# First loads of an attention and soft-MoE kernel split over two kinds of DMA queue, with products of zeros in TensorE's waits

## The chip, the cores and the metric

The kernel runs on one core of a Trainium2 chip. The metric is the device time of one execution in microseconds (us). Five runs of the kernel before gave a median of 154.34 us (153.34 to 154.71).

## The reference, cut to what matters

There are two stages. The first is attention over 4 batches of 8 heads, 768 tokens and 64 channels; each head is causal ("retrieval") or keeps only the first 4 tokens and a window of 64:

```python
scores = scale * np.matmul(q, k.transpose(0, 1, 3, 2))
mask = np.where(retr[0, :, 0, 0, None, None], full_mask, stream_mask)
scores = np.where(mask[None, :, :, :], scores, -1000000000.0)
a = softmax(scores)                      # over the last axis
attn_out = np.matmul(a, v)
```

The second takes the 3072 tokens x 512 channels that come out as `x` and runs a soft mixture of 8 experts with 4 slots each:

```python
logits = x @ phi                                        # 512 x 32
slot_input = softmax(logits, axis=0).T @ x              # 32 slots
slot_out[e] = np.maximum(slot_input[e] @ w1[e], 0.0) @ w2[e]   # 512 x 1024 x 512
out = softmax(logits, axis=1) @ slot_out
```

All inputs are float32 in HBM: q, k and v are 6.3 MB each, w1 and w2 16.8 MB each; the output is 6.3 MB.

## The kernel before, in words

**Attention.** The work goes by pairs of heads, n = 0 to 15 (four pairs a batch). A pair's q, k and v come as tiles of 96 partitions x 2 heads x 512 values: partition p holds tokens 8p to 8p+7. TensorE transposes them (`transpose`, line 73: 16 small products into one PSUM tile), an engine copies them out (`evac`, line 82), and v is turned back into token blocks (`v_blocks`). Within a pair the causal blocks are split into six groups (line 23). For each group g the loop issues the scores (`qk`, line 106: TensorE, then the exponential on ScalarE), and between them a list written out by hand (lines 413 to 474): masks on VectorE, the products with v (`pvmm`), the transposes of the next pair, and once per pair the division by the row sums (`norm`). The order on each engine is the order in which the program issues; nothing is moved by a scheduler. Group 0 of a pair needs only the token blocks 0 to 2 of q and 0 and 1 of k. Partitions 0 to 47 of a raw tile hold the blocks 0 to 2, partitions 48 to 95 the blocks 3 to 5.

**Loads.** From pair 1 on, loads are issued by GpSimd (`load`, line 65), whose DMAs can turn float32 into bfloat16 on the way (the queue that the profile calls software_dynamic, here SWDGE). They go three pairs ahead, into three buffers for each of q, k and v; one load must wait until the transposes of the pair that used its buffer are done. Between them GpSimd issues the sixteen weight loads of 2 MB each (`w_load`, line 271), about three for four pairs, and the six that are left at pair 13. At most eight of GpSimd's DMAs are outstanding: the ninth waits for the first. All of this is one queue.

**Pair 0** is different: `load_first` (line 55) has SyncE and ScalarE issue its loads (queues called hardware_dynamic, here HWDGE). [...]q, k and v land as float32 in memory that later holds the weights w2[7] and w2[6], and `cast` (line 363) turns them into bfloat16 on VectorE and ScalarE (lines 372 to 375 and 390). The flags `is_retrieval` come by ScalarE's queue (`ri`, line 327). While the data is on its way TensorE runs 20 products of a tile of zeros (`warm`, line 59), and 3 more after the first transposes; they write a scratch tile in PSUM that nobody reads. VectorE meanwhile computes what the masks of all heads are made from; `head_mask(h)` then makes head h's mask, for heads 0 and 1 in group 0, for the others at places listed in `MASK_AT`.

**The end.** After pair 15 the last token logits, `exp_tokens` and `slots_in` (lines 484 to 507) give the slots' inputs `siT`. `layer1` (512 x 1024 for each expert) and `layer2` follow on TensorE (lines 510 to 566), then the output: 24 products with `slot_out` (line 585), scaled on ScalarE and VectorE and written to HBM by SyncE (line 591) in nine DMAs.

Of the kernel before, what the change touches and what calls it, by code (L numbers as in the profile page):

```python
# [10 lines left out]
F32 = mybir.dt.float32  # L11
BF16 = mybir.dt.bfloat16
# [7 lines left out]
P = 128  # L20
# [9 lines left out]
MCOL = [0, None, 256]  # L30
NG = len(GROUPS)

MASK_AT = {(0, 1): 2, (0, 2): 3, (0, 3): 4, (0, 4): 5, (1, 1): 6, (1, 2): 7}


class Attn:
# [16 lines left out]
        self.xb, self.xT, self.expB, self.elg, self.lg = {}, {}, {}, {}, {}  # L53

    def load_first(self, w, eng, stage):
        self.rawt[w, 0] = self.raw.tile([P, 2, 512], BF16, tag=w + "r", name=w + "r")
        eng.dma_start(stage, self.src[w][0, 0:2].rearrange("h (p s) d -> p h (s d)", s=8))

    def warm(self, count):

        t = self.trp.tile([P, 256], F32, tag="tr", name="warm")
        for _ in range(count):
            self.nc.tensor.matmul(t, self.zeros[:, :P], self.zeros, start=True, stop=True)

    def load(self, n, which="qkv"):
        b, h = n // 4, 2 * (n % 4)
# [15 lines left out]
    def evac(self, n, w):  # L82
        tp = self.tp.pop((w, n))
        pool = self.vTp if w == "v" else self.qkT
        dst = pool.tile([P, 768], BF16, tag=w + "T", name=w + "T")
        o = dst.rearrange("c (j s p) -> c j s p", j=6, s=8)
        i = tp.rearrange("c (s j p) -> c j s p", j=6, s=8)
        if n == 0 and w == "q":
            self.nc.scalar.copy(o, i)
        else:  # L90
            self.nc.vector.tensor_copy(o, i)  # L91
        self.T[w, n] = dst

    def v_blocks(self, n):
# [149 lines left out]
def kernel(  # L244
# [24 lines left out]
    w2s = [singles.tile([P, 8, DM], BF16, name=f"w2_{e}") for e in range(NE)]  # L269
# [27 lines left out]
    with ExitStack() as actx:  # L297
        asing = actx.enter_context(tc.tile_pool(name="asing", bufs=1))
# [5 lines left out]
        ri = asing.tile([P, 2 * H], I32, name="ri")  # L304
# [16 lines left out]
        stage = [stage[:96, 1024 * i:1024 * (i + 1)].rearrange("p (h c) -> p h c", h=2) for i in range(2)]  # L321
        stage.append(w2s[NE - 2].rearrange("p a b -> p (a b)").bitcast(F32)[:96, :1024].rearrange(
            "p (h c) -> p h c", h=2))
# [7 lines left out]
        at.zeros = at.ptp.tile([P, 2, 512], BF16, tag="pT", name="zeros").rearrange("p a c -> p (a c)")[:, :256]  # L331
        nc.vector.memset(at.zeros, 0.0)
# [30 lines left out]
        def cast(w, i, part, eng):  # L363
            o, x = at.rawt[w, 0][:96, :, part], stage[i][:, :, part]
            if eng is nc.scalar:
                eng.copy(o, x)
            else:
                eng.tensor_copy(o, x)  # L368

        lo, hi = slice(0, 256), slice(256, 512)  # L370
# [13 lines left out]
        def head_mask(h):  # L384
            for c0, c1, r in ((0, 256, r0), (256, 640, r1)):
                nc.vector.tensor_scalar(msk[:, h, c0:c1], level[:, c0:c1], r[:, h:h + 1], 2.0,
                                        op0=ALU.add, op1=ALU.is_ge)

        at.evac(0, "k")
        cast("v", 2, slice(0, 512), nc.vector)  # L390
        wi = 0
        for n in range(NP):
            if n + 3 < NP:
# [14 lines left out]
            for g in range(NG):  # L408
                at.qk(n, g)
                last = n == NP - 1  # L410

                b, bt = (n - 4) // 4, (n - 4) % 4 if n >= 4 else 0
                if g == 0:
                    if n == 0:
                        at.transpose(0, "v")
                        head_mask(0)
                        at.evac(0, "v")
                        head_mask(1)

                        nc.vector.tensor_scalar(fb0, r0, 1.0, 30000.0, op0=ALU.subtract, op1=ALU.mult)  # L420
                        nc.vector.tensor_scalar(fb1, r1, 1.0, 30000.0, op0=ALU.subtract, op1=ALU.mult)
                    else:
                        at.pvmm(n - 1, 4)
                        at.v_blocks(n)
                        at.evac_blocks(n)
                    at.mask(n, 0)
                elif g == 1:
                    if n:
                        at.pvmm(n - 1, 5)
                    else:  # L430
                        at.v_blocks(n)
                        at.evac_blocks(n)
# [7 lines left out]
                elif g == 2:  # L440
                    if not last:
                        at.transpose(n + 1, "q")
                    at.pvmm(n, 0)
                    at.mask(n, 1)
                    if not last:
                        at.evac(n + 1, "q")
                elif g == 3:
                    if not last:
                        at.transpose(n + 1, "k")
                    at.pvmm(n, 1)  # L450
                    at.mask(n, 2)
                    if not last:
                        at.evac(n + 1, "k")
# [32 lines left out]
        at.x_transpose(n, range(3))  # L486
        at.evac_x(n, range(3))
        at.pvmm(n, NG - 1)
        at.norm(n, 1)
# [7 lines left out]
        at.token_logits(b, 1, range(3), (at.scp, "sc"))  # L497
        at.exp_tokens(b, 0, range(1))
        at.x_transpose(n, range(3, 6))
        at.evac_x(n, range(3, 6))  # L500
        at.slots_in(sip, b, range(3))
# [1 line left out]
        at.exp_tokens(b, 1, range(1))  # L503
        for c in range(2):
            at.exp_tokens(b, c, range(1, 4))
        at.slots_in(sip, b, range(3, 6))
        nc.vector.tensor_copy(siT, sip)
        hs, hT = {}, {}

        def layer1(e4, c):  # L510
# [59 lines left out]
    with tc.tile_pool(name="osb", bufs=8) as osb, \  # L570
         tc.tile_pool(name="ops", bufs=6, space=PSUM) as ops:
        for b in range(B):
# [4 lines left out]
            r = 0  # L577
# [50 lines left out]
```

The softmax here doesn't subtract the row's maximum and nothing guards it: scores larger than these inputs give would overflow.

## Time and profile before

| what | value |
|---|---|
| median of five runs | 154.34 us (153.34 to 154.71) |
| the profiled execution's own time | 154.49 us |
| its span, first to last instruction | 152.8 us |
| outside the span | 1.7 us |
| TensorE busy | 129.5 us (85%) |
| VectorE busy | 116.3 us (76%) |
| ScalarE busy | 112.5 us (74%) |
| first scores of pair 0 | at 9.37 us |
| slots' inputs `siT` ready for layer 1 | at 120.2 us |
| read from HBM | 52.5 MB |

The page gives busy time for each engine, the span in 40 slices with a digit for the busy tenths (`PEclk` is the TensorE clock that was granted, in tenths of full speed, `DMA` the busy share of the 16 DMA engines, `GB/s` what they wrote), DMA queues, the chain of work that ended last, and groups of instructions. A float32 that is turned into bfloat16 on the way counts with the bytes that are written, so 200 GB/s of such loads are 400 GB/s of reading.

### The profile page before, as it was taken

To read this page: it belongs to the slowest core of one execution; us is meant where nothing else is said; L and a number is where in the kernel's file an instruction comes from. 1 tells how busy PE (TensorE), PEld (TensorE's weight loads), DVE (VectorE), ACT (ScalarE), POOL (GpSimd) and SP (SyncE) were. 2 spreads that over 40 slices of the span, in tenths; PEclk is the share of its full clock that TensorE was granted. 3 is DMA by queue.
4 is the path that set the end of the run, shared out by engine and by line. 5 is a ranking of instruction groups with operands and counts; after the bars stand their busy time and mean duration, and the time that the engine had idled before them with its cause. 6 is when DMAs were issued, how large, how long until landed. Compare 5 with 4: busy or idle time off the path is not lost.

```text
span 152.8 us, 5568 instructions
## 1 busy us (share of the span) xinstructions
PE 129.5 (85%) x2398; PEld 86.7 (57%) x2398; DVE 116.3 (76%) x284; ACT 112.5 (74%) x176; POOL 40.5 (26%) x75
## 2 busy tenths in 40 slices
PE   7789989999799999999999999999977799399000
PEld 5546656667576675767667577766646348244000
DVE  6279799899988899898899989989976143189400
ACT  3146889999899899899989899989984262169200
POOL 7543563514336132433523335400000000000000
PEclk9999999999999999999999999999999699969975
DMA  4999999999999999999999999999999998149995
GB/s 118 226 209 208 228 191 229 198 227 193 214 222 195 227 195 228 195 215 220 198 224 200 221 194 214 225 212 217 219 212 214 214 214 172 36 173 405 412 418 240
DMA packets 14423, 33.51 MB, mean 219 GB/s; under 512 B 1856, under 2 KB 10496, under 8 KB 12480
## 3 DMA queue, kind: packets, MB, share of 16 engines
q0 software_dynamic: 11808, 25.63, 88.2%
q1 hardware_dynamic: 2240, 7.14, 12.8%
q10 hardware_dynamic: 352, 0.40, 1.0%
q8 instruction: 18, 0.29, 0.7%
q14 instruction: 5, 0.04, 0.1%
HBM read 52.50 MB, written 6.29 MB: 385 GB/s over the span
## 4 chain that ended last, share of the span: by engine, by line
DMA 53%; DVE 16%; PE 16%; issue 5%; POOL 2%; DVEq 0%; ACT 0%; ACTq 0%; POOLq 0%
DMA w<-in_moe_w_dram 33%; DMA kr<-in_k_dram 9%; DMA qr<-in_q_dram 7%; DMA ri<-in_is_retrieval_dram 4%; PE pv L149 4%; PE sc L114 4%; DVE ot L590 4%; DVE xb L162 3%; PE tpv L78 2%; DVE pT L136 2%; PE op L585 2%; DVE pT L133 2%; DVE vb L103 1%; POOL w L279 1%; DVE xT L176 1%
## 5 line engine op out<-in xcount | busy, mean ns | idle before, releaser
L123 ACT ACTIVATE pT<-sc,fb 128x512 bf16<-128x512 f32 (+1 forms) x96 | 52.6, 620 | 4.3 <-PE sc L114 2.9
L119 ACT ACTIVATE pT<-sc 128x1024 bf16<-128x1024 f32 (+1 forms) x48 | 44.8, 952 | 5.6 <-PE sc L114 4.9
L149 PE MATMUL pv<-vb,pT 128*128 128x65 bf16 x672 | 37.3, 196 | 3.9 <-DVE pT L133 2.3
L114 PE MATMUL sc<-qT,kT 64*128 64x256 bf16 (+3 forms) x320 | 36.0, 288 | 0.2 <-DVE kT L91 0.2
L149 PEld LDWEIGHTS <-pT 128*128 128x128 bf16 x672 | 26.6, 98 | 15.2 <-issue 6.3
L136 DVE TENSOR_TENSOR pT<-pT,msk 128x1024 bf16<-128x1024 bf16 (+1 forms) x32 | 19.7, 616 | 0.0
L162 DVE TENSOR_TENSOR xb<-pv,rs 128x384 bf16<-128x384 f32 x32 | 17.9, 558 | 1.1
L69 POOL DMA_DIRECT2D qr<-in_q_dram x15 | 9.7, 650 | 32.5 <-PE tpq L78 30.0
L114 PEld LDWEIGHTS <-kT 64*128 64x128 bf16 x320 | 10.4, 94 | 8.0 <-issue 1.5
L176 DVE COPY xT<-tpx 128x768 bf16<-128x768 bf16 (+1 forms) x17 | 9.1, 534 | 4.4 <-PE tpx L170 4.3
L69 POOL DMA_DIRECT2D vr<-in_v_dram x15 | 9.4, 630 | 10.7 <-PE tpv L78 10.7
L69 POOL DMA_DIRECT2D kr<-in_k_dram x15 | 9.5, 636 | 7.8 <-PE tpk L78 7.5
L133 DVE TENSOR_TENSOR pT<-pT,msk 128x1024 bf16<-128x1024 bf16 x16 | 10.9, 681 | 0.0
L78 PE MATMUL tpq<-ident,qr 96*64 96x96 bf16 x256 | 9.2, 218 | 1.0 <-DVE qr L368 1.0
L170 PE MATMUL tpx<-ident,xb 128*128 128x128 bf16 x96 | 8.2, 220 | 1.9 <-DVE xb L162 1.1
L91 DVE COPY vT<-tpv 128x768 bf16<-128x768 bf16 x16 | 8.8, 547 | 1.3 <-PE tpv L78 1.3
L78 PEld LDWEIGHTS <-qr 96*64 96x64 bf16 x256 | 6.9, 116 | 4.0 <-issue 2.5
L590 DVE TENSOR_SCALAR ot<-op,rrow 128x512 f32<-128x512 f32 (+1 forms) x13 | 8.6, 723 | 0.7 <-PE op L585 0.5
L78 PE MATMUL tpk<-ident,kr 96*64 96x96 bf16 x256 | 9.1, 218 | 0.0
L78 PE MATMUL tpv<-ident,vr 96*64 96x96 bf16 x256 | 9.1, 217 | 0.0
L103 DVE COPY vb<-tpb 128x768 bf16<-128x768 bf16 x16 | 8.9, 557 | 0.2 <-PE tpb L97 0.2
L78 PEld LDWEIGHTS <-vr 96*64 96x64 bf16 x256 | 6.9, 116 | 3.8 <-issue 3.4
(88 smaller groups left out, 158.0 us busy)
## 6 DMA issues: line engine op xcount, KB each, us to landing
w<-in_moe_w_dram POOLq DMA_DIRECT2D x15, 1024.0 KB, 14.7
out_dram<-ot SPq DMA_DIRECT2D x7, 768.0 KB, 6.3
qr<-in_q_dram POOLq DMA_DIRECT2D x15, 192.0 KB, 10.5
kr<-in_k_dram POOLq DMA_DIRECT2D x15, 192.0 KB, 9.8
vr<-in_v_dram POOLq DMA_DIRECT2D x15, 192.0 KB, 9.3
w<-in_moe_w_dram POOLq DMA_DIRECT2D x2, 512.0 KB, 33.9
out_dram<-ot SPq DMA_DIRECT2D x1, 512.0 KB, 2.7
w<-in_k_dram ACTq DMA_DIRECT2D x1, 384.0 KB, 5.7
```

The source lines that it names most:

```text
L69: self.nc.gpsimd.dma_start(t[:96], self.src[w][b, h:h + 2].rearrange("h (p s) d -> p h (s d)", s=8))
L78: self.nc.tensor.transpose(tp[64 * i:64 * (i + 1), s * 96:(s + 1) * 96], src[:96, i, s * 64:(s + 1) * 64], self.ident[:96, :96])
L103: self.nc.vector.tensor_copy(self.vbufs[n % 2][:, :, :, :64], tp.rearrange("p (j h d) -> p h j d", j=6, h=2))
L114: nc.tensor.matmul(sc[:, hh, c:c + ni * P], kT[po:po + 64, j * P:(j + 1) * P], qT[po:po + 64, i0 * P:(i0 + ni) * P], start=True, stop=True)
L119: nc.scalar.activation(pT[:, :, :L], sc[:, :, :L], ACT.Exp, scale=self.scale)
L123: nc.scalar.activation(pT[:, hh, :L], sc[:, hh, :L], ACT.Exp, scale=self.scale, bias=fb[:, h + hh:h + hh + 1])
L133: nc.vector.tensor_mul(v, v, m)
L136: nc.vector.tensor_mul(pT[:, :, :L], pT[:, :, :L], self.msk[:, h:h + 2, c:c + L])
L149: self.nc.tensor.matmul(self.pv[n, lo][:, hh, i % 3, :], pT[:, hh, o:o + P], vb[:, hh, j, :65], start=first, stop=True, skip_group_check=True)
L162: nc.vector.tensor_mul(xo, pv[:, :, :, :64], rs.to_broadcast([P, 2, 3, 64]))
L176: self.nc.vector.tensor_copy(self.xT[n // 4][:, n % 4, c], self.tp.pop(("x", n))[:, c])
L590: nc.vector.tensor_scalar_mul(ot[:, i, c0:c0 + cl], op[:, :cl], rr)
```

## The change

- `load_first` is called for q and k only. It loads partitions 0 to 47 (token blocks 0 to 2) of q by SyncE and of k by ScalarE, as float32 into staging memory, and partitions 48 to 95 by GpSimd, which casts on the way. These two GpSimd DMAs stand ahead of everything on its queue but the two iotas; the building of `ident` (a memset and a select) comes after them.
- v of pair 0 is loaded by GpSimd with `load`, ahead of pair 1. Its staging memory and its cast are gone, and so is the cast of the second half of q and k. `ri` moves from ScalarE's queue to SyncE's, behind q.
- The transposes of q and k of pair 0 come in two halves of 48 partitions (`transpose_first`, `evac_first`): the first halves before the loop, with 4 products of zeros after them instead of 3; the second halves in group 0, after the first scores, with 2 products of zeros after them. v's transposes move from group 0 to group 1 and its token blocks from group 1 to group 2; 2 more products of zeros stand in group 1. The masks of heads 2 to 7 move by one group.
- Before the loop VectorE's copy of kT no longer stands behind the instructions that read the flags.
- Products of zeros write a PSUM tile of their own (`waste`), so that they no longer wait for a copy.
- At the end the scores of the last batch's tokens with the first three of the four channel blocks of the first half move up ahead of the transposes of pair 15, and 10 products of zeros are spread over the waits up to layer 1.

```diff
-MASK_AT = {(0, 1): 2, (0, 2): 3, (0, 3): 4, (0, 4): 5, (1, 1): 6, (1, 2): 7}
+MASK_AT = {(0, 2): 2, (0, 3): 3, (0, 4): 4, (1, 1): 5, (1, 2): 6, (1, 3): 7}
...
+        t = self.raw.tile([P, 2, 512], BF16, tag=w + "r", name=w + "r")
+        src = self.src[w][0, 0:2].rearrange("h (p s) d -> p h (s d)", s=8)
+        eng.dma_start(stage, src[:48])
+        self.nc.gpsimd.dma_start(t[:48], src[48:96])
+        self.rawt[w, 0] = t
+
+    def transpose_first(self, w, late):
+        src, p0, n = self.rawt[w, 0], 0 if late else 64, 48
+        tp = self.trp.tile([P, 8 * n], BF16, tag="tr", name="tp" + w)
+        for s in range(8):
+            for i in range(2):
+                self.nc.tensor.transpose(tp[64 * i:64 * (i + 1), s * n:(s + 1) * n],
+                                         src[p0:p0 + n, i, s * 64:(s + 1) * 64],
+                                         self.ident[p0:p0 + n, p0:p0 + n])
+        self.tp[w, 0] = tp
...
-        at.load_first("q", nc.sync, stage[0])
-        at.load_first("k", nc.scalar, stage[1])
-        at.load_first("v", nc.sync, stage[2])
-        nc.scalar.dma_start(ri, bass.AP(tensor=ir32, offset=0, ap=[[0, P], [1, 2 * H]]))
         nc.gpsimd.iota(ki, pattern=[[0, 1]], base=0, channel_multiplier=1)
...
+        at.load_first("q", nc.sync, stage[0])
+        at.load_first("k", nc.scalar, stage[1])
+        nc.sync.dma_start(ri, bass.AP(tensor=ir32, offset=0, ap=[[0, P], [1, 2 * H]]))
...
+        at.load(0, "v")
         at.load(1)
         at.load(2)
...
-        cast("q", 0, lo, nc.vector)
-        cast("q", 0, hi, nc.vector)
-        cast("k", 1, lo, nc.scalar)
-        cast("k", 1, hi, nc.vector)
-        at.transpose(0, "q")
-        at.transpose(0, "k")
-        at.warm(3)
-        at.evac(0, "q")
+        nc.vector.tensor_copy(at.rawt["q", 0][64:112], stage[0])
+        nc.scalar.copy(at.rawt["k", 0][64:112], stage[1])
+        for w in "qk":
+            at.transpose_first(w, False)
+        at.warm(4)
+        at.evac_first("q", False, nc.scalar.copy)
+        at.evac_first("k", False, nc.vector.tensor_copy)
...
-        at.evac(0, "k")
-        cast("v", 2, slice(0, 512), nc.vector)
...
                     if n == 0:
-                        at.transpose(0, "v")
+                        for w in "qk":
+                            at.transpose_first(w, True)
+                            at.evac_first(w, True, nc.vector.tensor_copy)
+                        at.warm(2)
                         head_mask(0)
-                        at.evac(0, "v")
                         head_mask(1)
...
-        at.token_logits(b, 0)
+        at.token_logits(b, 0, range(3))
         at.token_logits(b, 1, range(3), (at.scp, "sc"))
+        at.x_transpose(n, range(3))
+        at.evac_x(n, range(3))
+        at.pvmm(n, NG - 1)
+        at.norm(n, 1)
+        at.waste = at.pvp.tile([P, 256], F32, tag="pv0", name="waste")
+        at.warm(2)
+        at.token_logits(b, 0, range(3, 4))
         at.exp_tokens(b, 0, range(1))
+        at.warm(4)
```

More of the change, by code (lines that the diff above doesn't have):

```diff
@@ L55, in load_first, with evac_first, warm @@
     def load_first(self, w, eng, stage):
[L56 to L61, printed above, removed]
+        t = self.raw.tile([P, 2, 512], BF16, tag=w + "r", name=w + "r")
[12 more added lines that the diff above has]
+        self.tp[w, 0] = tp
+    def evac_first(self, w, late, eng):
+        tp = self.tp.pop((w, 0))
+        if not late:
+            self.T[w, 0] = self.qkT.tile([P, 768], BF16, tag=w + "T", name=w + "T")
+        dst = self.T[w, 0][:, 384:] if late else self.T[w, 0][:, :384]
+        eng(dst.rearrange("c (j s p) -> c j s p", j=3, s=8), tp.rearrange("c (s j p) -> c j s p", j=3, s=8))
+    def warm(self, count, cols=256):
         for _ in range(count):
-            self.nc.tensor.matmul(t, self.zeros[:, :P], self.zeros, start=True, stop=True)
+            self.nc.tensor.matmul(self.waste[:, :cols], self.zeros[:, :P], self.zeros[:, :cols],
+                                  start=True, stop=True)
     def load(self, n, which="qkv"):
@@ L87, in evac @@
         i = tp.rearrange("c (s j p) -> c j s p", j=6, s=8)
[L88 to L91, printed above, removed]
+        self.nc.vector.tensor_copy(o, i)
         self.T[w, n] = dst
@@ L320 @@
         stage = w2s[NE - 1].rearrange("p a b -> p (a b)").bitcast(F32)
-        stage = [stage[:96, 1024 * i:1024 * (i + 1)].rearrange("p (h c) -> p h c", h=2) for i in range(2)]
-        stage.append(w2s[NE - 2].rearrange("p a b -> p (a b)").bitcast(F32)[:96, :1024].rearrange(
-            "p (h c) -> p h c", h=2))
-        at.load_first("q", nc.sync, stage[0])
-        at.load_first("k", nc.scalar, stage[1])
-        at.load_first("v", nc.sync, stage[2])
-        nc.scalar.dma_start(ri, bass.AP(tensor=ir32, offset=0, ap=[[0, P], [1, 2 * H]]))
+        stage = [stage[64:112, 1024 * i:1024 * (i + 1)].rearrange("p (h c) -> p h c", h=2) for i in range(2)]
         nc.gpsimd.iota(ki, pattern=[[0, 1]], base=0, channel_multiplier=1)
@@ L330 @@
         nc.gpsimd.iota(qi, pattern=[[128, 2], [1, 8], [8, 16]], base=0, channel_multiplier=0)
-        at.zeros = at.ptp.tile([P, 2, 512], BF16, tag="pT", name="zeros").rearrange("p a c -> p (a c)")[:, :256]
+        at.load_first("q", nc.sync, stage[0])
+        at.load_first("k", nc.scalar, stage[1])
+        nc.sync.dma_start(ri, bass.AP(tensor=ir32, offset=0, ap=[[0, P], [1, 2 * H]]))
+        at.zeros = asing.tile([P, 256], BF16, name="zeros")
+        at.waste = at.pvp.tile([P, 256], F32, tag="pv1", name="waste")
         nc.vector.memset(at.zeros, 0.0)
@@ L361 @@
         nc.vector.tensor_single_scalar(sink, kk, float(n_sink), op=ALU.is_lt)
[L363 to L370, printed above, removed]
-        cast("q", 0, lo, nc.vector)
-        cast("q", 0, hi, nc.vector)
-        cast("k", 1, lo, nc.scalar)
-        cast("k", 1, hi, nc.vector)
-        at.transpose(0, "q")
-        at.transpose(0, "k")
-        at.warm(3)
-        at.evac(0, "q")
+        nc.vector.tensor_copy(at.rawt["q", 0][64:112], stage[0])
[5 more added lines that the diff above has]
+        at.evac_first("k", False, nc.vector.tensor_copy)
         nc.vector.tensor_single_scalar(rne, ri.rearrange("p (h c) -> p h c", c=2), 0.0, op=ALU.not_equal)
@@ L430 @@
                     else:
-                        at.v_blocks(n)
-                        at.evac_blocks(n)
+                        at.transpose(0, "v")
+                        at.evac(0, "v")
+                        at.warm(2)
                     if bt == 1:
@@ L440 @@
                 elif g == 2:
+                    if n == 0:
+                        at.v_blocks(n)
+                        at.evac_blocks(n)
                     if not last:
@@ L485 @@
         at.pvmm(n, NG - 2)
[L486 to L489, printed above, removed]
         sip = at.scp.tile([P, 4, ES], F32, tag="sc", name="sip")
@@ L495 @@
                              skip_group_check=True)
-        at.token_logits(b, 0)
+        at.token_logits(b, 0, range(3))
         at.token_logits(b, 1, range(3), (at.scp, "sc"))
+        at.x_transpose(n, range(3))
[3 more added lines that the diff above has]
+        at.waste = at.pvp.tile([P, 256], F32, tag="pv0", name="waste")
+        at.warm(2)
+        at.token_logits(b, 0, range(3, 4))
         at.exp_tokens(b, 0, range(1))
+        at.warm(4)
         at.x_transpose(n, range(3, 6))
@@ L505 @@
             at.exp_tokens(b, c, range(1, 4))
+        at.warm(2)
         at.slots_in(sip, b, range(3, 6))
         nc.vector.tensor_copy(siT, sip)
+        at.warm(2)
         hs, hT = {}, {}
```

## The prediction, made before the changed kernel had run

> **What bounds the kernel now.** I read the page's slices first. TensorE, VectorE and ScalarE have idle tenths everywhere; the DMA row has none from the second slice to the 33rd.
>
> ```profile
> PEclk9999999999999999999999999999999699969975
> DMA  4999999999999999999999999999999998149995
> ...
> q0 software_dynamic: 11808, 25.63, 88.2%
> ```
>
> Then the chain that ended last, in order of time, and the waits of TensorE near the end:
>
> ```profile
> 97.90 34.68 DMA w<-in_moe_w_dram
> 132.58 0.04 issue
> 132.62 0.32 PE sp L545 x4
> ```
>
> ```profile
> PE sp L545 <- DMA w<-in_moe_w_dram: 2.1, 1, 2.1
> ```
>
> GpSimd issues its last weight load at 97.90 us; it lands 34.68 us later, at 132.58, because everything queued before it has to pass. TensorE is through with all that it has at 130.5 and waits 2.1 us for it. Nothing that follows can start earlier: last products, `slot_out`, output, 20.2 us to the end at 152.8. So the time is: the moment at which the input stream has passed, plus 20.2, plus 1.7 outside the span (154.49 in all; the median of the runs is 0.15 less). The inputs are the same bytes before and after. An edit counts only if it moves the end of that stream, or the 20.2 behind it. Attention is covered by 2.1 us of waiting; it gains nothing by being earlier.
>
> The stream is therefore looked at where it isn't full: its start. The DMA queues up to 6.6 us:
>
> ```profile
> q1 hardware_dynamic: 374, 0.73, 45.8%
> q10 hardware_dynamic: 298, 0.40, 21.9%
> ...
> qr<-in_q_dram POOLq DMA_DIRECT2D x2, 192.0 KB, 7.6
> ```
>
> and the first issues and products, from the timeline:
>
> ```profile
> 0.81 0.38 SPq L57 DMA_DIRECT2D w<-in_q_dram  x1
> ...
> 1.12 4.45 PE L63 MATMUL warm<-zeros 128*128 128x256 bf16 x20 [1.12 <-DVE zeros L332]
> ...
> 1.84 0.81 POOL L69 DMA_DIRECT2D qr<-in_q_dram  x1
> ...
> 6.62 0.87 PE L78 MATMUL tpq<-ident,qr 96*64 96x96 bf16 x16 [1.04 <-DVE qr L368]
> ...
> 9.37 0.61 PE L114 MATMUL sc<-qT,kT 64*128 64x256 bf16 x4 [0.20 <-DVE kT L91]
> ...
> 19.83 0.53 PE L78 MATMUL tpq<-ident,qr 96*64 96x96 bf16 x16
> ```
>
> There is no row for q0, GpSimd's queue: in 6.6 us it moved nothing, though its first DMA was issued at 1.84. All of the first 1.13 MB is HWDGE, and it is slow: the windows show 356 GB/s from 3 to 4 us, but 272, 230 and 173 in the next three.
>
> **The change, part by part.**
>
> *The stream.* Before: the first q0 load (192 KB, issued 1.84) lands 7.0 us after its issue, at 8.9. At the 187 to 210 GB/s of the windows from 7 to 10 us it takes 0.95 us, and a landing shows about 0.9 us after the last packet; so q0 starts at about 7.0 on an average engine, as HWDGE's 1.16 MB end. After: HWDGE has only 0.40 MB. By the windows that amount is through at 3.7 us (16 + 152 KB to 3.0, then 356 GB/s). The 0.77 MB moved to q0 write 384 KB, at 200 GB/s 1.9 us. If q0 starts when HWDGE is done, the place reached at 7.0 before is reached at 3.7 + 1.9 = 5.6 to 5.8: a gain of 1.2 us.
>
> Two things can spoil it. One is GpSimd's issuing. Iotas end at 1.37; two loads at 0.81 and 0.64 end at 2.85; `ident` (memset and select, 1.33 to 1.89 before) 0.56; v is issued at 3.4. If a load's packets come 1.0 us after its 0.64 of issuing, v's come at 5.05, while the two half loads (0.95 together) are through at 4.75: a gap of 0.3, and with 2 us from issue to packets 0.7. I take 0.3. The other is when q0 can start at all. The Trainium skill (DMA: Bandwidth & Descriptors, Latency and other measured facts) gives a first byte of about 1 us for SWDGE; the row says 4.8 us or more (issue 1.84, nothing by 6.6). By the rule q0 is ready at about 2.4 to 3.2, so the gain is whole; by the row, taken as a latency, q0 starts at 1.4 + 4.8 = 6.2, the DMA engines stand idle from 3.7 to 6.2, and the place is reached at 8.1 to 8.3: a loss of 1.2. I take the rule's side, since the trace has a reason for the late start: q0 appears just as v's last HWDGE packets leave, and the DMA share dips only to 0.81 between. A start hidden behind a full queue looks like this; a latency that ends just there would be chance. But one trace can't exclude it.
>
> So the stream: -1.2 + 0.3 = -0.9 us, between -1.2 and +1.3.
>
> *Behind the stream.* TensorE will reach its wait some 2 us earlier than before (below) and the last weights come only 0.9 earlier, so it stands idle longer and in two pieces. Before, the clock fell to 0.52 only in the window from 133 to 134, after the last 12 of the L545 products. After, I expect those to run at half clock. The price from the same kernel: 16 products of L516 take 1.90 us at clock 0.50 and 1.05 at full; so `slot_out`, which starts 0.34 after the first product, starts 0.3 later. From -0.1 (the clock can be luckier too) to +0.4; I take +0.3. The output itself writes at 412 GB/s and doesn't care.
>
> *Pair 0's compute.* Its data land at about 4.2 (q) and 4.5 (k), not 6.1 and 6.5. VectorE's cast of 1024 values 0.68 (row L368, v); ScalarE's about 1.1 (0.62 for half). q is transposed at 5.0 to 5.7, k from 5.6 to 6.3; 4 products of zeros at 0.22 (20 in 4.45) end at 7.2 and hide both copies (under 0.5 us each); the scores start at 7.2 or before, not 9.37. kT's copy no longer stands behind the flags, which landed at 8.0. These 2.2 us go to zero: they end in a longer wait at 130. A new wait is VectorE's: the second halves' copies stand ahead of masks 0 and 1 and hold them, and with them the mask of group 0, until q0's halves have landed (5.2 and 5.7 in the good case; 7.6 and 8.1 in the bad one, still earlier than 10.75, when group 1's scores start before). TensorE's queue behind the second transposes holds group 1's scores and v. Covered by the 2.1 us, and by 2.2 more.
>
> *Products of zeros, moved transposes and masks.* The same VectorE work is done but for three casts; 5 more products in the first 10 us and 10 at the end are 15 x 0.22 = 3.3 us of TensorE at most, in waits. They are meant to hold the clock. The skill's rule (TensorE: Matmul & The Clock Gate, Part 1) is that some 3.4 us of steady work raise the clock. The row speaks against it in this case: after 4.45 us of products without a gap, 16 transposes still take 0.87 us at 6.62, against 0.53 at 19.83; the page's 9 there is no evidence. By the rule pair 0's transposes would be 0.3 us shorter each, by the row nothing; at the end L516 would lose its 1.90 for 1.05. Either way it is TensorE that gets earlier at a wait for a DMA: 0. Were that cover gone, it would be worth up to 0.9 at the end.
>
> *GpSimd's queue.* Three DMAs more pass it, with at most eight outstanding: the ninth waits for the first half load. From 9 us on eight of them are over 3 MB, several us of stream; no gap follows. Cost 0.
>
> Sum: 154.49 - 0.9 + 0.3 = 153.9; 0.15 less for the median: 153.7.
>
> **The rivals.**
>
> - *SWDGE starts late* (slower). Place: q0 after the first GpSimd issue at 1.4. Price: +1.3 in the stream and +0.3 for the colder clock: 155.9. It decides if q0's first packets come after about 5 us, since 7.0 less 1.9 is where the two orders are level. For it: 4.8 us without a packet. Against it: the coincidence with the end of HWDGE, and a dip of the DMA share that is short. Chance 0.32.
> - *The whole gain.* q0 starts by 3.7, no gap, no cold clock: 154.34 - 1.2 = 153.1, to 152.7 if HWDGE's slow stretch of 4 to 7 us was the load of three queues. Chance 0.20.
> - *The stream isn't what matters*: attention's 2.2 us and the warmer clock come through, 154.34 - 2.2 = 152.1. The 34.68 us row and TensorE's wait speak against it: 0.01.
> - *Not what it says*: the gap and the cold clock eat the 1.2: 154.3, 0.05.
>
> **How the numbers follow.** The forecast (153.4 to 154.1 on its own) has 0.42. A measurement of this kernel can tell about 0.5%, 0.77 us; faster means below 153.57. Some 0.4 of the forecast's chance lies there (0.17), and in the two rivals below it (0.21): 0.38 in all. Same: the rest of the forecast and the eaten gain, 0.30. Slower: the late start, 0.32. To leave out no more than 2 in 10 the range must reach the late start: 152.7 to 155.9.
>
> **What would show it.** In the DMA queues of the first 5 us a row for q0 (its absence at 5 us means the late start). The first load of pair 1 lands near 7.9 rather than 8.9. The last weights land at 131.7, not 132.58, and TensorE's wait for them grows from 2.1 to 3 us or more. Scores of pair 0 by 7.2. L516's first 16 near 1.05. If the end of the weights doesn't move, or moves against the start of q0, the step on the stream is wrong; if the total falls by more than the weights' landing, the bound is.

## The result, and the profile after

| | before | after |
|---|---|---|
| median of the runs | 154.17 us (80 runs, 153.29 to 156.13) | 155.01 us (43 runs, 154.07 to 155.84) |
| profiled execution, own time | 154.49 us | 155.09 us |
| its span | 152.8 us | 153.4 us |
| first scores of pair 0 | 9.37 us | 7.57 us |
| last weights land | 132.58 us | 132.79 us |
| first output DMA issued | 134.74 us | 135.27 us |
| from there to the end of the span | 18.1 us | 18.1 us |

The ratio, which leaves out runs over 1.5% above the fastest of their kernel as a slower state, is 1.0048, with an interval of 1.0034 to 1.0061: the changed kernel is slower by half a per cent. (The two medians above stand at 1.0054.) The forecast was 153.7 us.

The page of the changed kernel first:

```profile
span 153.4 us, 5663 instructions
...
PEclk9965999999999999999999999999999999659955
DMA  5999999999999999999999999999999999149995
...
q0 software_dynamic: 12240, 26.02, 90.0%
...
q8 instruction: 19, 0.31, 0.7%
```

The DMA row is as full as before. In the clock row the 6 at 119 us is gone, and ahead of the output there is one slice more below 9 (65 where there was one 6). The 65 near the start only looks new. The kernel before has 9s there, but its products were slow until about 17 us: 16 transposes of 96 columns take 0.87 us at 6.62 and 0.53 at 19.83, and in the changed kernel 0.53 from 15.76 on. The chain of work that ended last, and the one row of TensorE's waits for a DMA, from 118 us on:

```profile
97.92 34.86 DMA w<-in_moe_w_dram
132.79 0.04 issue
132.83 0.85 PE sp L565 x10
```

```profile
PE sp L565 <- DMA w<-in_moe_w_dram: 3.9, 2, 2.2
```

Same bound, same shape: the last weight load is issued at 97.92 (97.90 before) and lands 34.86 us later (34.68). TensorE now waits 3.9 us for the two last loads, in two pieces, where it waited 2.1 in one. All that attention gained is in this wait. The timeline shows the pieces, and the windows show the clock over them (the columns are busy time by engine, then PEclk, DMA share and GB/s):

```profile
130.38 0.29 PE L565 MATMUL sp<-w,hT 128*32 128x256 bf16 x4 [1.73 <-DMA w<-in_moe_w_dram]
132.83 0.83 PE L565 MATMUL sp<-w,hT 128*32 128x256 bf16 x12 [2.15 <-DMA w<-in_moe_w_dram]
...
135.27 1.29 SPq L611 DMA_DIRECT2D out_dram<-ot  x2
```

```profile
130.00:132.00 2.00, 0.29 (x4) 0.10 (x4) 0.00 (x0) 0.00 (x0) 0.00 (x0) 0.93 0.41 84
132.00:134.00 2.00, 1.02 (x13) 0.57 (x13) 0.29 (x1) 0.47 (x1) 0.00 (x0) 0.50 0.02 4
134.00:136.00 2.00, 1.93 (x6) 0.74 (x5) 1.40 (x4) 0.97 (x2) 0.00 (x0) 0.50 0.00 0
```

The same windows of the kernel before:

```profile
132.00:134.00 2.00, 1.02 (x15) 0.71 (x15) 0.48 (x1) 0.58 (x2) 0.00 (x0) 0.76 0.00 0
134.00:136.00 2.00, 2.00 (x6) 0.65 (x5) 1.73 (x3) 1.23 (x3) 0.00 (x0) 0.50 0.18 72
```

The clock is down to 0.50 when the last 12 products start, so they take 0.83 us for 0.51, and from the landing to the first output DMA it is 2.48 us for 2.16. So the 0.6 us of span are 0.2 of stream and 0.3 of cold clock; the rest is an output 0.1 longer, and rounding.

Now the start. DMA queues of the changed kernel up to 6.6 us, with three of its loads (KB each, median us from issue to landing):

```profile
q0 software_dynamic: 398, 0.37, 41.1%
q1 hardware_dynamic: 382, 0.22, 18.9%
q10 hardware_dynamic: 112, 0.20, 13.6%
...
w<-in_k_dram ACTq DMA_DIRECT2D x1, 192.0 KB, 4.7
w<-in_q_dram SPq DMA_DIRECT2D x1, 192.0 KB, 4.5
...
qr<-in_q_dram POOLq DMA_DIRECT2D x1, 96.0 KB, 4.6
```

GpSimd's queue, of which there was no row before, has moved 0.37 MB by 6.6 us, and its half load lands 4.6 us after its issue, as fast as HWDGE's. Its first packet runs at 3.5 us, 2.0 after the issue; in the kernel before the first one ran at 6.7, 4.8 after the issue, as HWDGE's ended. So it was not late. The timeline:

```profile
1.50 0.71 POOL L61 DMA_DIRECT2D qr<-in_q_dram  x1
...
2.21 0.57 POOL L61 DMA_DIRECT2D kr<-in_k_dram  x1
...
3.31 0.67 POOL L91 DMA_DIRECT2D vr<-in_v_dram  x1
...
6.02 0.43 PE L69 MATMUL tpq<-ident,qr 48*64 48x48 bf16 x16 [0.46 <-DVE qr L381]
...
7.57 0.39 PE L133 MATMUL sc<-qT,kT 64*128 64x256 bf16 x4
```

The scores come 1.8 us earlier, 16 transposes of 48 take 0.43 us, and the clock stays full until 8.8 us. But the rate of the stream is lower. Windows of the kernel before from 8 to 11 us, and then of the changed one from 4 to 6 and from 8 to 11 (last column GB/s written; nearly all of it is cast on the way here, so twice that is read):

```profile
8.00:9.00 1.00, 0.75 (x7) 0.35 (x3) 0.89 (x4) 0.33 (x1) 0.73 (x2) 1.00 1.29 206
9.00:10.00 1.00, 0.80 (x7) 0.17 (x8) 1.00 (x3) 0.00 (x0) 0.32 (x1) 1.00 1.40 210
10.00:11.00 1.00, 1.00 (x20) 0.77 (x20) 0.48 (x3) 0.98 (x1) 0.00 (x0) 1.00 1.43 215
```

```profile
4.00:5.00 1.00, 1.00 (x7) 0.69 (x6) 0.00 (x0) 0.00 (x0) 1.00 (x2) 1.00 1.12 150
5.00:6.00 1.00, 0.56 (x3) 0.09 (x1) 0.69 (x1) 0.43 (x1) 1.00 (x2) 1.00 0.96 128
...
8.00:9.00 1.00, 1.00 (x36) 0.69 (x34) 0.81 (x4) 0.99 (x1) 0.37 (x1) 0.92 1.12 173
9.00:10.00 1.00, 1.00 (x20) 0.73 (x18) 1.00 (x6) 0.54 (x2) 0.88 (x2) 0.50 1.07 162
10.00:11.00 1.00, 1.00 (x12) 0.30 (x8) 1.00 (x4) 0.51 (x1) 0.39 (x1) 0.50 1.20 181
```

Summing the packets of the trace, with a packet that is cast counted twice, gives what had been read by a given time, in KB. Four kernels of the experiments are put beside:

| by | before | after | e2 | e18 | e5 | e13 |
|---|---|---|---|---|---|---|
| 7 us | 1202 | 1259 | 1277 | 1261 | 1344 | 1371 |
| 12 us | 3175 | 2979 | 3040 | 3039 | 3262 | 3297 |
| 120 us | 48270 | 48028 | 48096 | 48089 | 48338 | 48366 |

The changed kernel leads by 57 KB at 7 us, is 196 behind at 12 and 242 at 120: 0.6 us at the 417 KB per us of the stretch from 12 to 120 us. What is lost in the first 12 us is not made up by 120. At the landing of the last weights only 0.2 us of it is left; there the DMA engines are full in neither kernel (a share of 0.55 from 129 to 130 us before, 0.80 after).

The first load of pair 1, which comes behind the same data of pair 0 in both, shows the lag too. Its row, first before (DMA issues from 1.8 to 2.0 us), then after (3.9 to 4.4):

```profile
qr<-in_q_dram POOLq DMA_DIRECT2D x1, 192.0 KB, 7.0
```

```profile
qr<-in_q_dram POOLq DMA_DIRECT2D x1, 192.0 KB, 6.1
```

Issued at 1.84 and 3.97 us, it lands at 8.88 before and at 10.05 after. This is not one execution's chance. Every kernel of the experiments below has one profile. In the eight with the old loads (the kernel before among them) this load lands at 8.6 to 9.0 us and 3132 to 3212 KB are read by 12 us. In the seven with the changed loads as they stand it lands at 9.3 to 10.3, and 2891 to 3040 KB are read.

### The profile page after: what moved, and what is told of

The parts are those of the page before. It is cut to its first block, busy times and chain, and to the rows that moved or that the text cites. A ratio compares the mean times of both kernels' runs of the same rounds, so it can differ in the third digit from the quotient of the medians.

```text
span 153.4 us, 5663 instructions
## 1 busy us (share of the span) xinstructions
PE 131.0 (85%) x2445; PEld 87.5 (57%) x2445; DVE 116.1 (76%) x283; ACT 112.5 (73%) x176; POOL 42.1 (27%) x78
## 4 chain that ended last, share of the span: by engine, by line
DMA 35%; DVE 27%; PE 19%; ACT 8%; issue 3%; POOL 1%; DVEq 0%; POOLq 0%; ACTq 0%
DMA w<-in_moe_w_dram 23%; DMA vr<-in_v_dram 9%; DVE xb L181 5%; PE pv L168 4%; DVE pT L155 4%; ACT pT L142 4%; PE sc L133 4%; DVE pT L152 3%; DMA w<-in_k_dram 3%; DVE ot L610 3%; DVE vb L122 3%; PE op L605 3%; DVE xT L195 3%; PE tpx L189 2%; PE tpv L100 2%
## 5 line engine op out<-in xcount | busy, mean ns | idle before, releaser
L181 DVE TENSOR_TENSOR xb<-pv,rs 128x384 bf16<-128x384 f32 x32 | 17.8, 558 | 1.1
L91 POOL DMA_DIRECT2D vr<-in_v_dram x16 | 10.4, 649 | 9.2 <-PE tpv L100 9.2
L605 PE MATMUL op<-slot_out,expT 128*128 128x512 bf16 (+1 forms) x25 | 8.6, 468 | 0.2
L608 ACT ACTIVATE ot<-op,rrow 128x512 f32<-128x512 f32 (+1 forms) x12 | 7.3, 668 | 2.0 <-PE op L605 1.6
L84 PE MATMUL waste<-zeros 128*128 128x256 bf16 x38 | 7.8, 357 | 1.1 <-DVE zeros L349 1.1
```

What stands on the lines that cost most here:

```text
L91: self.nc.gpsimd.dma_start(t[:96], self.src[w][b, h:h + 2].rearrange("h (p s) d -> p h (s d)", s=8))
L181: nc.vector.tensor_mul(xo, pv[:, :, :, :64], rs.to_broadcast([P, 2, 3, 64]))
```

## The experiments

All ratios are to the kernel before, run on the same chip, with 95% intervals.

**Which half.** The changed kernel's end in the kernel before, and the changed kernel's head with the old end (everything from the end of the loop over pairs to `layer1` taken from the other kernel).

```diff
 e1: before, and behind the loop:
+        at.token_logits(b, 0, range(3))
...
+        at.warm(2)
 e2: after, without these lines
```

> The kernel before with the end of the changed one: moved token logits and 10 products of zeros, loads untouched. Theory S (the input stream ends no earlier, because the loads that went to SWDGE lost their time again in the first 12 us): 154.2, no change. Theory C (what is lost is lost behind the stream: TensorE comes earlier to its wait for the last weights, sits idle longer and runs the output's products at half clock): TensorE is about 1 us earlier at its wait, so 154.4 to 154.6. Theory A (attention and the end decide, so an end that is 1 us shorter shows): 153.2.

> The changed kernel with the end of the one before: only the loads and the start are changed. S: the loss is in the loads, so all of it stays: 154.9 to 155.0. C: TensorE comes about 1 us later to its wait than in the changed kernel but still 1 us earlier than before, so between: 154.5 to 154.8. A: slower than the changed kernel by 1 us: 156.

e1 took 1.0084 (1.0059 to 1.011), e2 1.0045 (1.0018 to 1.0072). So the head alone has a loss as large as the whole change's. The end by itself loses too, which I had not expected; but its profiled execution has its last products at 132.41 and its first output DMA at 134.43, both ahead of before. It loses inside the output, by something that the changed kernel doesn't have there (below).

**The cold clock.** Products of zeros in TensorE's two last waits: 12 and 16 of them in the changed kernel, 14 in the kernel before.

```diff
                 for fo in range(8):
...
+                    if e == NE - 1 and c == 0 and fo in {0: 12, 4: 16}:
+                        for _ in range({0: 12, 4: 16}[fo]):
+                            nc.tensor.matmul(waste, at.zeros[:, :P], at.zeros, start=True, stop=True)
```

> The changed kernel with 12 and 16 products of zeros in TensorE's two waits for the last weights (1.3 and 1.7 us of 1.7 and 2.2 us). S: the clock is a side effect worth nothing, 155.0. C: the granted clock stays at 1.0 past the landing, the output starts 0.3 to 0.5 us earlier: 154.4 to 154.7. If the products are too many they end after the landing and cost up to 0.5 us instead.

> The kernel before with 14 products of zeros in TensorE's wait for the last weights (1.5 of 2.1 us). S: 154.2. C: before too lost one window of half clock, 133.05 to 136.46, so 153.8 to 154.0, faster than both kernels.

e3, timeline:

```profile
131.21 1.92 PE L567 MATMUL wasteL<-zeros 128*128 128x256 bf16 x16
133.29 0.51 PE L568 MATMUL sp<-w,hT 128*32 128x256 bf16 x12 [0.16 <-DMA w<-in_moe_w_dram]
...
135.31 1.01 SPq L615 DMA_DIRECT2D out_dram<-ot  x2
```

The clock holds: 0.51 us for the 12 products, and 2.06 us from the landing (133.25) to the output's first DMA, 0.42 less than in the changed kernel. But in this execution the weights landed 0.46 later, and over 22 runs the ratio is 1.0053 (1.003 to 1.0077). The cold clock is real and costs 0.3 to 0.4 us of one execution; taking it away isn't seen in the median. e9: 1.0146 (1.0096 to 1.0196); its zeros ended 0.9 us after the landing (133.44 for 132.50), and it had the output's trouble as well.

**The order of GpSimd's issues.** In e5 v's load is issued ahead of `ident` (2.77 us for 3.31). e4 holds phi's small packets back. e13 is e5 with e3's zeros.

```diff
 e5, e13:
+        at.load(0, "v")
         nc.sync.dma_start(ri, bass.AP(tensor=ir32, offset=0, ap=[[0, P], [1, 2 * H]]))
...
-        at.load(0, "v")
 e4:
+                nc.vector.memset(phf[:, :, :1], 0.0)
                 nc.sync.dma_start(phf, moe_phi.rearrange("(do di) s -> di do s", di=P))
```

> The changed kernel with v's load of pair 0 ahead of ident on GpSimd's queue. S (the gap of 5.0 to 5.7 us in the SWDGE stream, while v's descriptors were still to come, is part of the loss): the gap closes, the stream gains 0.2 us: 154.8. C: 155.0. If ident then comes late, TensorE's first transposes wait for it and nothing is lost behind TensorE's waits: 154.8 to 155.0 as well.

> The changed kernel with one edit: the load of phi (512 packets of 128 bytes, which ran among the first SWDGE loads from 6 to 10 us) waits for an instruction of VectorE in pair 1, at about 17 us. Theory S1 (phi's small packets hold up the young SWDGE stream): the first loads of pair 1 land by 9 us in all engines, the stream is 0.3 us ahead at 12 us, 154.7. Theory S2 (phi costs the same wherever it runs): 155.0. Theory C (clock behind the stream): 155.0.

> The changed kernel with v's load ahead of ident and with 12 and 16 products of zeros in the last waits. S: v ahead brought 0.3 (155.0 to 154.8) and the zeros nothing: 154.7. C and S together: 0.4 more: 154.3. A gain over the kernel before, 153.7, needs both in full and the 19th block away from the last weights.

e5: 1.0023 (0.9998 to 1.0047), windows:

```profile
8.00:9.00 1.00, 1.00 (x34) 0.87 (x32) 0.43 (x2) 0.76 (x1) 0.00 (x0) 0.50 1.22 197
9.00:10.00 1.00, 1.00 (x14) 0.33 (x10) 0.93 (x5) 0.27 (x1) 0.88 (x2) 0.50 1.18 180
10.00:11.00 1.00, 1.00 (x21) 0.69 (x18) 1.00 (x6) 0.69 (x1) 0.38 (x1) 0.50 1.22 198
```

With this one line moved the stream is 87 KB ahead of the kernel before at 12 us instead of 196 behind. The profiled execution's span is 151.9 us, but it is the lowest of the 22, and the median is not below before's. By the ratios about half of the loss comes back, though the two intervals overlap. e13: 1.0029 (1.0007 to 1.0051), with the best stream of all in its profiled execution and again the lowest of its runs there. Three pairs differ in v's place alone: the changed kernel and e5, e3 and e13, and e16 and e17 below. In each the ratio is 0.0023 to 0.0025 lower with v ahead, some 0.4 us, though in none are the intervals apart, and by the medians of all runs e13 is not below e3. e4: 1.0087 (1.0057 to 1.0118); phi now lands so late that VectorE waits for it (the load has 7.7% of the chain), and its profiled execution, at 158.87 us, is the longest of its runs, so it says nothing of the time. By 12 us it reads 2948 KB. Leaving phi's 65 KB out of the changed kernel's 2979, it is 34 KB ahead, of the 196 lost; so the burst of small packets is at most a small part of what slows the stream.

**How much stream is in the way.** Both kernels without the load of w2[7]; expert 7 uses w2[6] instead, so 2.1 MB, some 5 us of stream, are left out.

```diff
-                if wi < 2 * NE:
+                if wi < 2 * NE - 1:
...
-                                     w2s[e][:, fo, c * 256:(c + 1) * 256], start=(e == 0 and fo < 4),
+                                     w2s[min(e, NE - 2)][:, fo, c * 256:(c + 1) * 256], start=(e == 0 and fo < 4),
```

> The kernel before without the load of w2[7], the last 2 MB of weights; expert 7's second layer uses w2[6]. This takes about 4.9 us off the stream. If the stream bounds, the time falls until TensorE's own work does: by the 2.1 us that it waited and the cold clock of 0.3 to 0.5, to 151.5 to 152.2. If attention and the end bound it (A), it stays at 154.2.

> The changed kernel without the load of w2[7]; expert 7's second layer uses w2[6]. With the stream taken off, what the change earned in TensorE's own work shows: TensorE was through 1.9 us earlier (128.66 against 130.53). S and C: 149.6 to 150.5, so 1.5 to 2 us faster than the same cut in the kernel before. If the changed start earned nothing in attention: the same as that cut, 151.5 to 152.2.

e7: 0.9932 (0.9906 to 0.9959). e8: 0.9734 (0.9689 to 0.9779). The kernel before gains at most 1 us (0.68%) from 5 us of stream, and that figure rests on the 8 fastest of 20 runs; the median of all 20 is 154.16 for before's 154.29. Its engines are hardly ahead of the stream. e7's last products:

```profile
130.09 2.80 PE L545 MATMUL sp<-w,hT 128*32 128x256 bf16 x96
```

Without a wait they end at 132.89, only 0.24 earlier than in the profile of before. The changed kernel goes from 1.0048 to 0.9734, 4.8 us, though by two runs (149.84 and 150.88; two more took 152.33 and 152.89). In the profiles e8's first output DMA is issued at 131.44, e7's at 134.40. So the changed compute is shorter by up to 3 us, and the stream hides it.

**Instructions come by DMA too.** The queue called q8 instruction moves blocks of 16 KB, one for some 260 of TensorE's instructions, each a single packet that takes 0.9 us or more. The profile of the kernel before has 18 such blocks for its 4798 TensorE instructions, that of the changed one 19 for 4892 (counted in the built program). Where does the 19th fall? (The second number of `warm` is the columns of a product, 256 without it.)

```diff
 e10:  -at.warm(20)   +at.warm(10, 512)                       4778 instructions
 e11:                 +at.warm(10, 32)                        4818
 e14:  -at.warm(20)   +at.warm(67, 80)                        4892
 e12:  the changed kernel without any product of zeros        4816
 e15, e16, e17: before, after and e5 with layer 2 in products
       of 512 columns, half as many                           4670, 4764, 4764
```

> The kernel before, with the same 4.45 us of zeros at the start made from 10 products of 512 columns instead of 20 of 256: 20 TensorE instructions fewer, nothing else. Theory I (TensorE's instructions are fetched in blocks of 16 KB[...], by the same DMA engines; what counts is where the 19th block falls: at the very end before, so in some executions inside the output): the 19th is never fetched, 153.6 to 154.1 and less scatter. Theories S and C: no change, 154.2.

> The kernel before, with 10 products of zeros of 32 columns more at the start (0.6 us, before the first data land): 20 TensorE instructions more. Theory I: the 19th block is fetched at about 136 us, inside the output, which ends when the slowest DMA engine does: 155.0 to 155.4, as with the moved end alone (155.23). S and C: no change, 154.2.

> The changed kernel without any product of zeros (38 fewer, 76 instructions): the loads, the halves and the order stay. Theory I: the 19th block moves from 131 us, TensorE's wait, to about 136 us inside the output: 155.5 to 156. Theory C (clock): TensorE is cold for longer at the start and later at its last wait, 155.0 to 155.3. If the products were themselves the cost: 154.2.

> The kernel before with its 20 products of zeros of 256 columns made into 67 of 80 columns, the same 4.45 us: 94 TensorE instructions more, as many as the changed kernel has more. Theory I (fetch): the 19th block comes at about 131 us, in the last of the weights, or in the output in some executions: 154.7 to 155.2 with much scatter, as the changed kernel (155.01, 154.07 to 155.84). S and C: 154.2, no change.

> The kernel before with the second layer's products 512 columns wide instead of two of 256: 128 TensorE instructions fewer (4670), same arithmetic. Theory I: no 19th block, as with 20 fewer: 154.0 with little scatter; up to 0.2 more because slot_out starts when all columns are done. S, C: 154.2.

> The changed kernel with the same wide second layer (4764 instructions): no 19th block. Theory I: the scatter goes and the time falls from 155.0 to 154.2 to 154.5; against e15 what is left is S and C, 0.2 to 0.5. If S and C are the whole loss: 155.0, 0.8 to 1.0 above e15.

> The changed kernel with v ahead of ident and the wide second layer. By the traces its stream is 0.6 us ahead of the changed kernel's at 12 us. Theory I with S: 153.5 to 153.8, faster than the kernel before and than e15. If v ahead earns nothing outside the profiled execution: as e16.

| | ratio | last block fetched at | first output DMA to the end |
|---|---|---|---|
| e1 | 1.0084 (1.0059 to 1.011) | 136.1 to 137.6 | 19.0 us |
| e9 | 1.0146 (1.0096 to 1.0196) | 136.4 to 137.8 | 18.9 |
| e11 | 1.0074 (1.0048 to 1.01) | 135.6 to 137.3 | 19.3 |
| e12 | 1.0122 (1.0082 to 1.0161) | 137.5 to 138.4 | 19.5 |
| e10 | 0.9981 (0.9967 to 0.9995) | 131.1 to 132.1 | 17.7 |
| e14 | 0.9989 (0.9973 to 1.0006) | 134.5 to 135.6 | 17.7 |
| e15 | 1.0006 (0.9985 to 1.0026) | 131.2 to 132.1 | 18.1 |
| e16 | 1.008 (1.0051 to 1.0109) | 127.4 to 128.4 | 17.7 |
| e17 | 1.0057 (1.0034 to 1.0081) | 129.0 to 130.0 | 17.8 |
| after | 1.0048 (1.0034 to 1.0061) | 131.5 to 132.4 | 18.1 |

Ten tiny products of zeros at the start of the kernel before (e11) cost 1.2 us at its other end. Its queues from 134 us on have a row that neither the kernel before nor the changed one has there:

```profile
q8 instruction: 1, 0.02, 0.5%
```

and its rate of moving, in 40 slices of the same stretch, has a tail:

```profile
GB/s 0 0 0 365 397 377 377 12 348 418 406 406 406 393 393 406 455 393 442 406 430 418 393 393 418 442 406 418 406 442 418 406 393 430 356 25 25 0 0 0
```

The last two slices, 1 us, run at 25 GB/s, a sixteenth of the 400 before them: one of the 16 engines is still at work when the others are done. One block falls into the output, holds up the engine that moves it, and the output, which is spread over all of them, ends over 1 us later. Without a block in it the output takes 17.7 to 18.1 us, with one 18.9 to 19.5. That accounts for e11's loss and most of e1's, for 0.8 us of e9's 2.3 and 1.4 of e12's 1.9. It does not explain the change: the changed kernel's last block comes at 131.5, in TensorE's wait; as many instructions in the kernel before cost nothing (e14); and with no 19th block in either profile the loss stays (e16 at 1.008 beside e15 at 1.0006). My theory that the fetch was the changed kernel's loss fell here.

The kernel before stands on the edge, though. e7 and e18 (below) have exactly its 4798 TensorE instructions and show a 19th block all the same: in e7 at 145.2 us, inside the output, which takes 19.3 us; in e18 at 153.2, behind it. So a part of e7's small gain, and of the long runs of the kernel before, can be a block in the output.

e14 and e10 show another thing. e14's products of layer 2:

```profile
131.01 2.96 PE L545 MATMUL sp<-w,hT 128*32 128x256 bf16 x96
```

All 96 in one row, without a wait: in this execution TensorE, not the stream, came last, at a time of 154.89 us. In e10's and e7's it is the same. The 2.1 us of waiting in the profile of before are one execution's.

**Loads or order.** e18 is the kernel before with the changed loads alone. e19 is the changed kernel with q, k and v whole by HWDGE.

```diff
 e18, load_first:
-        eng.dma_start(stage, self.src[w][0, 0:2].rearrange("h (p s) d -> p h (s d)", s=8))
...
+        eng.dma_start(stage, src[:48])
+        self.nc.gpsimd.dma_start(self.rawt[w, 0][48:96], src[48:96])
 e19, load_first:
-        self.nc.gpsimd.dma_start(t[:48], src[48:96])
+            eng.dma_start(stage[:48], src[48:96])
```

> The kernel before with the changed kernel's loads alone: the first 48 partitions of q and k by HWDGE, the other 48 and v by SWDGE, ident built after the two half loads, the flags on SyncE's queue. The order of transposes, masks and products of zeros stays as before. My theory is that the loads cost what the changed kernel lost, by a stream that is some 0.5 us behind from 12 us on: ratio to before 1.003 to 1.006 and less read by 12 us than before's 3187 KB. The rival is that the new order in pair 0 (and the scatter that comes with it) costs it: then this kernel is within 0.15% of before.

> The changed kernel with the kernel before's loads: q, k and v of pair 0 whole by HWDGE as float32, ident built first, the casts of q's and k's second halves and of v on VectorE; the halves in the transposes, the order and the products of zeros stay as changed. If the loads are the loss: ratio to before 0.998 to 1.002. If the order in pair 0 or the products at the end are: 1.004 or more. TensorE has as many instructions here as in the changed kernel, so the fetch of its instructions is no difference.

e18: 1.0082 (1.0057 to 1.0107). The loads alone lose, without any of the new order, and by more than the whole change; its stream lags like e2's (table above), and its last wait is in two cold pieces like the changed kernel's:

```profile
130.41 0.29 PE L544 MATMUL sp<-w,hT 128*32 128x256 bf16 x4 [1.88 <-DMA w<-in_moe_w_dram]
132.42 0.83 PE L544 MATMUL sp<-w,hT 128*32 128x256 bf16 x12 [1.71 <-DMA w<-in_moe_w_dram]
```

So the new order is not what costs; if anything it gives some back. But e18's profile does not show how the 1.2 us are lost: its last weights land at 132.38 us, earlier than before's. e19: 1.007 (1.0034 to 1.0106), which by its own forecast would blame the new order; but it answers another question. Its timeline:

```profile
9.44 0.17 DVE L393 TENSOR_SCALAR rne<-ri 128x16 f32<-128x16 int32 x1 [2.19 <-DMA ri<-in_is_retrieval_dram]
...
10.72 0.62 PE L71 MATMUL tpq<-ident,qr 48*64 48x48 bf16 x16 [3.01 <-DVE qr L403]
```

With five larger loads in the HWDGE queues the flags land only at 9.4 us, VectorE stands before the casts, TensorE 3 us before the second halves, and with them stand the buffers and the loads that wait for them. TensorE's last wait for the weights is 0.25 us. That is a new wait of the experiment's own, and e19 tells nothing of the loads.

## Why the prediction was wrong

- *The bound* (input stream, then 20.2 us): right for the two profiled executions. The chain is the same, attention's 1.8 us went into the wait, and e8 beside e7 shows up to 3 us of shorter compute that the stream hides. In other executions of kernels like the one before (e7, e10, e14) TensorE came last.
- *When GpSimd's queue starts*: right. It started 2.0 us after its issue, not 4.8; the rival that made it late is out. The Trainium skill's 1 us (DMA: Bandwidth & Descriptors, Latency and other measured facts) is nearer than the row was, and still too short.
- *The stream term, "-1.2 + 0.3 = -0.9 us"*: this step failed, in its -1.2. It had HWDGE's half loads through at 3.7 us and GpSimd's queue writing 200 GB/s from then on. The half loads landed at 5.3 and 5.5 us, not at 4.2 and 4.5, and GpSimd's queue, alone by then, wrote 128 GB/s from 5 to 6 us. So the place that the kernel before reaches at 7.0 us, which was to be reached at 5.6 to 5.8 plus a gap of 0.3, is reached at 6.8. And from there the stream was to run at before's rate. From 7 to 12 us it reads 344 KB per us; before reads 395. By the prediction's own sign, the first load of pair 1 landed at 10.05 us, not near 7.9. Instead of 0.9 us gained, the stream is 0.6 us behind at 120 us and the weights land 0.2 later. I had taken the 200 GB/s from a queue that had been given six loads before its first packet ran, and used it for one that ran from its first load on. e18's ratio says that the loads alone lose. e5 points to where a part of the lag comes from: with v 0.54 us earlier, ahead of `ident`, the place is reached at 6.5 (so the gap of 0.3 was priced right), the rate from 7 to 12 us is 384, and the stream doesn't fall behind. e13 shows the same. e17, with v in the same place, is level with the kernel before by 12 us (3163 KB), at a rate of 362, and its ratio is 1.0057 all the same. All three are profiles of the lowest of their runs, and the ratios give back only half. So v's late issue, which I priced as a gap and nothing more, is a part of the error and perhaps not all.
- *The cold clock, +0.3*: right in size (2.48 us for 2.16), with the longer wait in two pieces that it named (3.9 us).
- *Pair 0's compute worth 0*: right. The scores came at 7.57, predicted 7.2, in part by luck: the data landed 1 us later than said, and the transposes were shorter.
- *The rule of the Trainium skill on the clock (TensorE: Matmul & The Clock Gate, Part 1) against the row*: the rule held in the changed kernel, the row in the kernel before. Behind 4.44 us of products of zeros the clock was full for pair 0's first transposes (16 of 48 columns in 0.43 us, 0.62 at half clock in e19), and fell again at 8.8 us. In the kernel before, 4.45 us of the same products had not raised it (0.87 us at 6.62). No run here shows what makes the difference. The first 16 products of layer 1 went from 1.90 to 1.05 us as the rule had it. Both went into the wait.
- *Cover of 2.1 us*: one execution's number. e7 gives 1 us at most, and e10 and e14 have executions without any.

That 155.01 us lies inside the stated range of 152.7 to 155.9 is luck. The range reached that far up for a late start of GpSimd's queue, and that did not happen.

What stays open: the profiled executions explain 0.6 us of the changed kernel's 0.84 between medians, but of e18's 1.2 us next to nothing, since its profiled execution (154.59 us) is among the lowest of its 19 runs. Kernels with split loads scatter more (the middle half of the runs spans 1.0 us in the changed kernel and in e5, 0.5 in the kernel before), and what differs between their executions isn't shown. Nor is it shown where the last instruction block falls in executions that have no profile: in e18 a block in the output is a rival for a part of its loss, and a version of e18 with fewer instructions, which would settle it, was not run. Nor is it shown why a load issued 0.54 us earlier raises the rate for the next 5 us.

No kernel here is clearly better than the kernel before; e10, at 0.9981, is the only one whose interval lies wholly below 1 without leaving anything out.

## What to carry to other kernels

Where one input stream bounds a kernel, a load that is moved from one queue to another gains only if the new queue keeps the DMA engines as full as the old one did: add up the bytes read by a fixed time (here 12 us), not the time at which the first data arrive. On the queue that carries the stream, it can pay to let nothing that isn't a load stand between the first loads: here 0.54 us of other work cost some 0.4 us by the ratios, in no pair clear of the noise. And a wait seen in one profile is not a cover for all executions: leave the waited-for load out once and see how much is gained.

## What the runs showed of the hardware

- Instructions share the DMA engines with data. A block of 16 KB holds some 260 of TensorE's instructions (18 blocks for 4798, 19 for 4892) and takes 0.9 to 1.7 us of one engine. Whether it falls into a wait or into the output is worth 1 us or more: 20 instructions more at the start of the kernel before cost 1.2 us (e11), 94 more nothing (e14).
- A load of 192 KB that GpSimd's queue casts to 96 landed 4.6 us after its issue, one of 192 KB by HWDGE, issued 0.7 us before it, 4.5; the casting queue costs nothing in the first landing, but the stream behind it read 344 KB per us instead of 395.
- In TensorE's last waits a clock of 0.50 came back with idle pieces of 1.7 and 2.15 us, and stayed away when products of zeros filled them (e3).
